# Gated MLP with linear attention on one core: gates of two token chunks kept in SBUF, tiles from any of three pools, refitted tables

## The chip, the core and the metric

The kernel runs on one core of a Trainium2 chip. The metric is the device time of one execution in microseconds (us). The core has five engines with a queue each: TensorE (PE in the profile; its weight loads are PEld), VectorE (DVE), ScalarE (ACT), GpSimd (POOL) and SyncE (SP), which here does nothing but issue DMAs. ScalarE issues some DMAs too.

## The reference

With S = 2048 tokens, width D = 640, 32 heads of 20, and F = 1536:

```python
xn = layernorm(x)
q, k, v = split_heads(xn @ wqkv)
phi = lambda t: concat([softmax(t @ w_phi), softmax(-(t @ w_phi))])    # per head
o = phi(q) @ (phi(k).T @ v) / (phi(q) @ phi(k).sum(tokens) + 1e-6)
s = merge_heads(o) @ wo
g = silu(gelu(xn @ w1 + b1) @ w2 + b2)
out = x + s * g
```

All in fp32. The output is written transposed, D rows by S columns.

## The kernel before

Every fp32 operand of a matmul is kept as a high and a low half (tiles of shape P x 2 x n), and a product is three matmuls over these halves (`PASSES`). Making the low half means one subtraction: "bank" copies the source to PSUM by ScalarE and subtracts on VectorE from PSUM; "vector" subtracts on VectorE from SBUF; "pool" on GpSimd from SBUF. The tokens are four chunks (c = 0 to 3) of CW = 512 columns, the output rows five blocks (d = 0 to 4) of 128.

The stages by the profiled execution's span: projections and the kv state to about 240 us; then `up` for chunks 2 and 3 (UP0) to 313, `down(2)` for the same chunks (DN0) to 396, `up` for chunks 0 and 1 (UP1) to 471, `down(0)` (DN1) to 550, and the output stage (OUT) to 648. Both MLP products are in Strassen-like forms: block sums of hr and of w2 are multiplied and the products added with signs. `form` (L1428) makes the operand hs of a product from the gelu results hr, six steps ahead; `step` calls it.

From UP0 on the order of every instruction is written out by hand: a counter of slots goes up with each `tick`, and `when`, `soon` and `after` put a call into a slot. The numbers come from the table `PLAN`. UP0, DN0, UP1, DN1 and OUT begin at slots 0, 42, 84, 126 and 168. A number like 165.25 is slot 165, behind what stands at 165.0 there. Each engine then works through its own queue in that order, and SyncE's queue holds most DMAs: a DMA that has to wait for its data holds back every DMA behind it on that queue.

In `down`, `gate_out` finishes a block of the MLP: it adds on VectorE what is needed (L1333), applies Silu on ScalarE (L1544) into a tile y, and a store to `g_dram` is issued on SyncE (all DMAs through `load` have line L1353). In the output stage `gate(i)` (L1789) loads the block back into a tile gt from the pool "cells". `load_res` (L1784) loads the matching block of x into xres.

In between, the attention's q side is prepared per token tile of 128 (16 tiles, four to a chunk), as `plan_q` orders it: `q_load` (eq), `q_ez` on GpSimd (L1667), `q_rc` (L1671), `q_dn`, which is a chain of six instructions on VectorE (L1677 to L1684), `q_scale` on GpSimd (L523), two transposes on VectorE (L1695) into a tile pt, and `q_put2`, which stores pt to `phi_dram` in four DMAs per half. `get_phi` loads them back as six tiles ph per chunk. `num_step` (six calls per chunk; num(c) below) multiplies these by the kv state (L1747, L1755) into PSUM banks, and ScalarE and VectorE write the halves of oT (L1751, L1752, and for the sixth part oTl L1760, L1761). A `spread`, a DMA of 32 KB on ScalarE's queue (L1764), moves a part of oTl into each of the five oT tiles.

`finish(c, d)` takes 15 matmuls of oT and wo per tile (L1815), multiplies gt by the bank on VectorE (L1817, two halves), adds xres on GpSimd (L1818; on VectorE for the last two tiles), and a store to the output follows.

Tiles come from pools with a fixed number of buffers: "slabs" (10), "cells" (21), "halves" (6), "late" (13, opened after UP1) and "phs" (1). A new tile of a pool waits for the readers of the tile that had its buffer. Before the change every kind of tile has one pool: oT, oTl, gt and hs come from cells, q tiles from late once it is open, and ph from late or slabs by the chunk (`c_ph`).

Of the kernel before, what the change touches and what calls it, by code (L numbers as in the profile page):

```python
# [15 lines left out]
P = 128  # L16
# [25 lines left out]
def _ft(t):  # L42
# [27 lines left out]
        [26.75, 31.75, 34.25, 35, 40],  # L70
        [38, 40, 43.0, 44, 45],
# [3 lines left out]
        [41.5, 41.5],  # L75
        [40, 42],
        [40.5, 45.25],
        [38, 43.5],
        [40.75, 45.5],
        [71.75, 74.0],  # L80
        [66, 73],
        [71.5, 76],
        [35, 35.5],
        [35.5, 37.5],
        [37.75, 38.75],
# [6 lines left out]
        [135.5, 156],  # L92
# [51 lines left out]
    "phi": [
        [152.5, 153.75, 158.0, 160.5, 160.0, 158.0],
        [161.5, 166.6, 161.7, 169.3, 169.9, 169.0],
        [176.5, 176.6, 176.7, 177.8, 174.9, 179.0],
        [184.25, 187.6, 187.7, 187.8, 187.9, 191.0],
    ],
    "num": [165.25, 173.5, 184.75, 194.25],  # L150
    "res": [166.25, 164, 171.25, 172.5, 172, 175.25, 175.5, 176.75, 184, 180.5, 180.5, 186, 186, 194, 191.75, 193.75, 195.75, 200, 196.5, 202],
    "gate": [167.1, 167.1, 168.1, 170.1, 168.6, 172.1, 176.1, 178.1, 180.1, 182.1, 185.1, 183.1, 190.85, 190.1, 192.1, 194.1, 195.1, 200.1, 199.1, 200.6],
    "c_ph": ['late', 'slab', 'late', 'slab'],
    "st": [3, 3, 4.75, 3, 4, 3, 3, 3, 3, 3, 3, 3, 5, 4, 4, 6, 3, 3, 3.75, 3],
    "c_st": ['scalar', 'sync', 'sync', 'sync', 'sync', 'sync', 'sync', 'sync', 'sync', 'sync', 'sync', 'scalar', 'scalar', 'sync', 'sync', 'sync', 'sync', 'scalar', 'sync', 'scalar'],
# [4 lines left out]
def hedgehog_gated_mlp_kernel(ctx: ExitStack, tc: tile.TileContext, x, xt_in, wqk, bd, wv, wo, w1, b1, w2, b2, out_t):  # L160
# [31 lines left out]
    open_psum(early_psum, A=3, T=1)  # L192
# [3 lines left out]
    def slab(dt, name, shape=(P, 2, D)):  # L196
        pool = slabs if next(homes, "S") == "S" else lead
        return pool.tile(list(shape), dt, tag="S", name=name)
# [939 lines left out]
    o = 7  # L1138
# [183 lines left out]
    halves = ctx.enter_context(tc.tile_pool(name="halves", bufs=6, reuse_waits="tile"))  # L1322
    ffn = ExitStack()
    ffn.enter_context(tc.manual_schedule())

    def cell(shape, dt, name):
        return cells.tile(list(shape), dt, tag="C", name=name)

    def half(name, shape=(P, CW)):
        return halves.tile(list(shape), F32, tag="U", name=name)  # L1330

    def add(out, a, b, eng=nc.vector, op=OP.add):
        eng.tensor_tensor(out, a, b, op=op)  # L1333
# [115 lines left out]
    W2AT = dict(A11=0, A21=2 * P, A12=4 * P, A22=6 * P, A5=8 * P)  # L1449
    SUMS = ("S2", "S3", "S4", "S1")  # L1450
# [78 lines left out]
    def down(c0, los):  # L1529
# [197 lines left out]
    def get_phi(c, n):  # L1727
        assert {("phi", c, u, h) for u in range(2) for h in range(2)} <= seen
        j = (5, 0, 1, 2, 3, 4)[n]
        if j == 5:  # L1730
            t = tailp[1].tile([P, CW], F32, tag="H", name="ph")
            load(t[:80], phi_dram[c, 1200:])
        else:
            w = PLAN["c_ph"][c]
            t = (cell((P, 2, CW), F32, "ph") if w == "cell" else
                 slab(F32, "ph", (P, 2, CW)) if w == "slab" else tall(F32, "ph", (P, 2, CW)))
            load(t[:], phi_rows(c, 240 * j))
        phis[c][j] = t
# [43 lines left out]
    xres, gates, wo_s, wo_r = {}, {}, [], []  # L1782
# [6 lines left out]
    def gate(i):  # L1789
        c, d = divmod(i, KC)  # L1790
        assert ("g", d, c) in seen
        gates[c, d] = cell((P, CW), F32, "gt")
        nc.sync.dma_start(gates[c, d][:], g_dram[d][:, c])
# [186 lines left out]
```

## Time and profile before

| | us |
|---|---|
| median of 3 runs | 649.2 (648.74 to 651.68) |
| the profiled execution's own time | 649.97 |
| its span | 648.1 |
| mean granted TensorE clock | 0.996 |
| TensorE busy | 625.4 |
| DMA moved | 155.26 MB, mean 240 GB/s |

The rows of the profile name an engine, a line of the kernel, the operation, "out<-in" with the names of tiles, and partitions x elements. In a timeline a row has its start, its length, how many instructions were joined in it (x12), and in brackets how long the engine sat idle before it and what ended that. In the table of waits a row has the sum, the number of times and the longest.

### The profile page before, as it was taken

How to read it: one execution, taken by the hardware profiler on the slowest of the kernel's cores; microseconds unless marked ns; L12 is line 12 of the kernel's file. 1: busy time of each engine (PE TensorE's matmuls, PEld its weight loads, DVE VectorE, ACT ScalarE, POOL GpSimd, SP SyncE). 2: the span in 40 equal slices, each digit the busy share in tenths (PEclk: the TensorE clock that was granted, in tenths of full speed). 3: DMA queues.
4: the chain of work that ended last, by engine and by line, in shares of the span. 5: the costliest groups of instructions: out<-in, count | busy, mean ns of one | idle time of the engine just before them, and what ended most of it. 6: DMA issues, size and time to landing. Idle time of an engine off the chain costs nothing.

```text
span 648.1 us, 11723 instructions
## 1 busy us (share of the span) xinstructions
PE 625.4 (97%) x4288; PEld 538.8 (83%) x4288; DVE 460.1 (71%) x706; ACT 365.8 (56%) x639; POOL 440.6 (68%) x390
## 2 busy tenths in 40 slices
PE   8999999999999999999989899999999999799997
PEld 8999999999899998888768688888788886466666
DVE  5878997766785767746688966889889973753242
ACT  4556877754476769877977476342597474121020
POOL 3597887775775439987799785666679977332332
PEclk9999999999999999999999999999999999989999
DMA  8436822132723858998999899967476998999974
GB/s 322 190 104 223 268 71 83 42 103 83 223 80 124 300 204 306 364 329 305 304 411 268 241 322 373 413 194 210 116 235 213 340 324 284 279 286 311 305 252 176
DMA packets 129609, 155.26 MB, mean 240 GB/s; under 512 B 48176, under 2 KB 89648, under 8 KB 129040
## 3 DMA queue, kind: packets, MB, share of 16 engines
q1 hardware_dynamic: 128656, 152.81, 70.7%
q10 hardware_dynamic: 896, 1.70, 0.7%
q8 instruction: 34, 0.56, 0.4%
q14 instruction: 23, 0.19, 0.1%
HBM read 98.96 MB, written 53.54 MB: 235 GB/s over the span
## 4 chain that ended last, share of the span: by engine, by line
PE 64%; POOL 12%; DMA 11%; issue 3%; DVE 3%; SPq 3%; ACT 2%; POOLq 0%
PE pB L1312 21%; PE pW L606 20%; PE pB L1523 6%; PE pB L1815 6%; PE pA L465 4%; POOL hr L1425 4%; DMA out_dram<-xres 3%; PE pW L1089 3%; DMA ph<-phi_dram 2%; POOL ez L1667 2%; SPq L1353 2%; DMA xp<-xp_dram 2%; PE pA L284 2%; DMA eq<-e_dram 1%; POOL eq L523 1%
## 5 line engine op out<-in xcount | busy, mean ns | idle before, releaser
L1523 PE MATMUL pB<-hs,w2s 128*128 128x512 f32 x648 | 149.1, 390 | 5.1 <-DVE hs L1443 2.9
L1523 PEld LDWEIGHTS pB<-hs,w2s 128*128 128x128 f32 x648 | 121.2, 188 | 32.8 <-DVE hs L1443 3.3
L1312 PE MATMUL pB<-xp,w1s 128*128 128x512 f32 x324 | 79.8, 390 | 0.8 <-DVE pB L1333 0.8
L1312 PE MATMUL pB<-xd,w1s 128*128 128x512 f32 x324 | 79.4, 389 | 0.0
L1815 PE MATMUL pB<-oT,wo 128*128 128x512 f32 (+1 forms) x315 | 70.7, 383 | 2.1 <-DMA oT<-oTl 2.1
L1312 PEld LDWEIGHTS pB<-xp,w1s 128*128 128x128 f32 x324 | 60.7, 188 | 13.8 <-DVE pB L1333 1.2
L1815 PEld LDWEIGHTS pB<-oT,wo 128*128 128x128 f32 x315 | 56.3, 188 | 18.1 <-issue 6.0
L1312 PEld LDWEIGHTS pB<-xd,w1s 128*128 128x128 f32 x324 | 60.8, 188 | 12.5
L1818 POOL TENSOR_TENSOR xres<-gt,xres 128x256 f32<-128x256 f32 x36 | 25.6, 735 | 59.3 <-DVE gt L1817 49.3
L1380 ACT ACTIVATE hr<-pB,b1t 128x512 f32<-128x512 f32 x48 | 32.6, 687 | 52.0 <-DVE pB L1333 51.6
L504 POOL TENSOR_TENSOR e<-e,mxs 128x1280 f32<-128x1280 f32 x12 | 28.8, 2408 | 40.4 <-DVE mxs L499 36.0
L1443 DVE TENSOR_TENSOR hs<-pB,hs 128x512 fp32r<-128x512 f32 x59 | 39.0, 679 | 19.0 <-ACT hs L1439 19.0
L1439 ACT ACTIVATE hs<-hr 128x512 fp32r<-128x512 f32 x84 | 50.7, 622 | 3.1 <-DMA s_dram<-ws 1.7
L1438 ACT ACTIVATE pB<-hr 128x512 f32<-128x512 f32 x59 | 34.9, 592 | 24.4 <-DVE rc L1684 12.6
L510 ACT ACTIVATE e<-e 128x1280 f32<-128x1280 f32 x32 | 40.7, 1273 | 13.6 <-POOL e L504 5.7
L606 PE MATMUL pW<-wsum,xd 128*128 128x320 f32 x288 | 48.4, 310 | 0.0
L1425 POOL TENSOR_TENSOR hr<-hr 128x512 f32<-128x512 f32 x36 | 47.5, 1346 | 1.2 <-DVE hs L1443 1.1
L606 PEld LDWEIGHTS pW<-wsum,xd 128*128 128x128 f32 x288 | 43.6, 188 | 0.0
L1817 DVE TENSOR_TENSOR gt<-pB,gt 128x256 f32<-128x256 f32 x40 | 15.2, 418 | 38.7 <-PE pB L1815 28.9
L523 POOL TENSOR_TENSOR e<-e,rc 128x1280 f32<-128x1280 f32 x15 | 36.1, 2409 | 5.8 <-DVE rc L950 4.3
L1667 POOL TENSOR_TENSOR ez<-eq,zrep 128x1280 f32<-128x1280 f32 x12 | 35.5, 2961 | 5.5 <-DMA eq<-e_dram 5.5
L1333 DVE TENSOR_TENSOR pB<-u,pB 128x512 f32<-128x512 f32 x36 | 24.7, 687 | 12.0 <-PE pB L1312 11.7
(244 smaller groups left out, 1366.2 us busy)
## 6 DMA issues: line engine op xcount, KB each, us to landing
w2s<-s_dram SPq DMA_DIRECT2D x24, 512.0 KB
e_dram<-e SPq DMA_DIRECT2D x16, 640.0 KB
ph<-phi_dram SPq DMA_DIRECT2D x20, 512.0 KB
raw<-in_w_dram SPq DMA_DIRECT2D x24, 320.0 KB
eq<-e_dram SPq DMA_DIRECT2D x12, 640.0 KB
phi_dram<-pt SPq DMA_DIRECT2D x48, 160.0 KB
w_dram<-w1s SPq DMA_DIRECT2D x12, 512.0 KB
s_dram<-ws SPq DMA_DIRECT2D x12, 512.0 KB
```

The costliest lines, as they stand in the source:

```text
L510: nc.scalar.activation(ef, ef, AF.Exp)
L523: eng.tensor_tensor(e3, e3, rc[:, :, None].to_broadcast([P, 64, DH]), op=OP.mult)
L606: nc.tensor.matmul(self.bank[ch][:, :HALF], self.x(blk, a), w(b), start=new and i == 0, stop=i == len(mms) - 1, skip_group_check=True)
L1312: nc.tensor.matmul(bank[ch][:], tl[:, a, off + wo_:off + wo_ + P], mov(blk, b), start=new and n == 0, stop=n == len(mms) - 1, skip_group_c ...
L1380: nc.scalar.activation(dst, ps, AF.Gelu_apprx_tanh, bias=b1t[:, f:f + 1])
L1425: nc.gpsimd.tensor_tensor(block(k, g), block(a, g), block(b, g), op=OP.subtract)
L1438: nc.scalar.activation(ps[:], src, AF.Copy)
L1439: nc.scalar.activation(hs[:, 0], src, AF.Copy)
L1443: (nc.gpsimd if lo == "pool" else nc.vector).tensor_tensor(hs[:, 1], ps[:] if lo == "bank" else src, hs[:, 0].bitcast(F32), op=OP.subtract)
L1523: nc.tensor.matmul(ps[:], w(b), hs[:, a, :], start=start and n == 0, stop=stop and n == 2, skip_group_check=True)
L1667: nc.gpsimd.tensor_tensor(qz[t], qe[t], zf[0], op=OP.mult)
L1815: nc.tensor.matmul(ps[:, cols], w, o[:, a, cols], start=n == 0, stop=n == 14)
```

## The change

1. Gates of chunks 0 and 1 stay in SBUF. `gate_out` with c0 == 0 writes its sums and Silu into one of five tiles ys (P x 2 x CW, one per d), and `gate` has nothing to load for c < 2. Ten stores to `g_dram` and ten loads from it, of 256 KB each, are no longer there, and `finish` multiplies into ys. The five tiles take their room from late, which has 9 buffers for 13.
2. Pools as rings. `from_ring` takes the first of several pools whose oldest tile is no longer held by the program that writes the instructions; ph, oT, gt, and the q tiles use it.
3. `PLAN` is refitted: slots of nearly all kinds, and for some tiles which engine makes the low half. In the first list of `lo` (the forms of DN0) entry 10 goes from bank to vector and entry 18 from pool to vector; in the second (DN1) entry 17 from vector to bank and entry 33 from pool to bank.

```diff
+    class Ring:
+        def tile(self, shape, dt, name, tag=None):
+            t = Tile(self.pool.tile(list(shape), dt, tag=self.tag, name=name))
+            self.given.append(weakref.ref(t))
+            return t
+        def ready(self):
+            return len(self.given) < self.n or self.given[-self.n]() is None
+    def from_ring(names, shape, dt, name):
+        names = [n for n in names if n in rings]
+        for n in names:
+            if rings[n].ready():
+                return rings[n].tile(shape, dt, name)
+        return rings[names[0]].tile(shape, dt, name)
...
         def gate_out(d, o, src, plus=None, late=1):
+            if c0 == 0:
+                if d not in ys:
+                    ys[d] = tailp[2].tile([P, 2, CW], F32, tag="Y", name="ys")
+                y = gates[o, d] = ys[d][:, o]
+                if plus is not None:
+                    add(y, src, plus)
+                    src = y
+                nc.scalar.activation(y, src, AF.Silu, bias=b2t[:, d:d + 1])
+                return
             y = half("y")
...
     def tall(dt, name, shape=(P, 2, D)):
-        if tailp:
-            return tailp[0].tile(list(shape), dt, tag="L", name=name)
-        return slab(dt, name, shape)
+        return from_ring(("late", "slab"), shape, dt, name)
...
     def new_oT():
-        return [cell((P, 2, 512), F32R, "oT") for _ in range(5)], cell((P, 2, 512), F32R, "oTl")
+        return [from_ring(("cell", "slab", "late"), (P, 2, 512), F32R, "oT") for _ in range(5)], cell(
+            (P, 2, 512), F32R, "oTl")
...
     def gate(i):
         c, d = divmod(i, KC)
-        assert ("g", d, c) in seen
-        gates[c, d] = cell((P, CW), F32, "gt")
-        nc.sync.dma_start(gates[c, d][:], g_dram[d][:, c])
+        if c >= 2:
+            assert ("g", d, c) in seen
+            t = from_ring(("cell", "slab", "late"), (P, CW), F32, "gt")
+            nc.sync.dma_start(t[:], g_dram[d][:, c])
+            gates[c, d] = t[:]
...
-    "num": [165.25, 173.5, 184.75, 194.25],
+    "num": [163.75, 173.5, 185.0, 194.25],
...
-    tailp.append(ctx.enter_context(tc.tile_pool(name="late", bufs=13, side="right", reuse_waits="tile")))
+    tailp.append(ctx.enter_context(tc.tile_pool(name="late", bufs=9, side="right", reuse_waits="tile")))
+    rings["late"] = Ring(tailp[0], 9, "L")
     tailp.append(ctx.enter_context(tc.tile_pool(name="phs", bufs=1, side="right", reuse_waits="tile")))
+    tailp.append(ctx.enter_context(tc.tile_pool(name="ys", bufs=5, side="right", reuse_waits="tile")))
```

How the order moves is shown at three places. First SyncE's queue at the end of DN1 and the beginning of OUT, before; L1353 is any load or store through `load`, L1787 the load of x, L1793 the load of a gate:

```order
L1353 DMA ph<-phi_dram 80x512
L1353 DMA ph<-phi_dram 128x2x512
L1353 DMA g_dram<-y 128x512 x3
L1787 DMA xres<-in_xt_dram 128x512 x2
L1353 DMA phi_dram<-pt_5978 32x20x64 x4
...
L1353 DMA g_dram<-y 128x512 x2
L1793 DMA gt<-g_dram 128x512 x4
L1353 DMA ph<-phi_dram 128x2x512 x3
L1793 DMA gt<-g_dram 128x512
```

And after, where L1387 stands for L1353 and L1830 for L1787:

```order
L1387 DMA ph<-phi_dram 80x512
L1387 DMA ph<-phi_dram 128x2x512
L1387 DMA phi_dram<-pt_5990 32x20x64 x4
L1830 DMA xres<-in_xt_dram 128x512 x2
L1387 DMA ph<-phi_dram 128x2x512 x3
L1383 DMA out_dram<-xres 128x512
L1830 DMA xres<-in_xt_dram 128x512 x3
```

The five stores of y and the first four gate loads no longer stand between the stores of pt_5978 (now pt_5990) and the three ph loads that follow.

Second, TensorE from DN1 into OUT, before: L1523 are the products of down, L1755 and L1747 those of num, L1815 those of the output:

```order
L1523 MATMUL pB<-hs,w2s 128x512 x312
L1755 MATMUL pB<-ph,bdl 40x256 x2
L1747 MATMUL pB<-ph,bdk 64x512 x10
L1523 MATMUL pB<-hs,w2s 128x512 x12
L1815 MATMUL pB<-oT,wo 128x512 x38
...
L1815 MATMUL pB<-oT,wo 128x512 x82
...
L1815 MATMUL pB<-oT,wo 128x512 x75
```

And after, with L1558, L1797, L1789 and L1860 for these four:

```order
L1558 MATMUL pB<-hs,w2s 128x512 x300
L1797 MATMUL pB<-ph,bdl 40x256 x2
L1789 MATMUL pB<-ph,bdk 64x512 x10
L1558 MATMUL pB<-hs,w2s 128x512 x24
L1860 MATMUL pB<-oT,wo 128x512 x38
...
L1860 MATMUL pB<-oT,wo 128x512 x90
...
L1860 MATMUL pB<-oT,wo 128x512 x67
```

num(0) stands 12 matmuls earlier, num(1) where it was, and num(2), between the 90 and the 67, 8 matmuls later.

Third, VectorE in DN0, where u is copied from the first product's bank, before:

```order
L1468 TENSOR_TENSOR w2s<-pB,w2s 128x2x256 x2
L1677 TENSOR_REDUCE pB<-qroom 128x64
L1680 SCALAR_TENSOR_TENSOR pB<-rc,pB 128x32
L1681 TENSOR_TENSOR pB<-pB,rc 128x64
L1682 TENSOR_REDUCE pB<-pB 128x32
L1683 RECIPROCAL pB<-pB 128x32
L1684 TENSOR_TENSOR rc<-rc,pB 128x64
L1566 COPY u_4140<-pB 128x512
L1443 TENSOR_TENSOR hs<-pB,hs 128x512
```

And after, with L1610 for the copy, L1719 to L1726 for the chain and L1477 for the forms:

```order
L1503 TENSOR_TENSOR w2s<-pB,w2s 128x2x256
L1610 COPY u_4130<-pB 128x512
L1477 TENSOR_TENSOR hs<-hr,hs 128x512
L1719 TENSOR_REDUCE pB<-qroom 128x64
L1722 SCALAR_TENSOR_TENSOR pB<-rc,pB 128x32
L1723 TENSOR_TENSOR pB<-pB,rc 128x64
L1724 TENSOR_REDUCE pB<-pB 128x32
L1725 RECIPROCAL pB<-pB 128x32
L1726 TENSOR_TENSOR rc<-rc,pB 128x64
```

The copy of u moved from behind the chain `q_dn` to ahead of it, and the form that follows reads both its operands from SBUF (hr), where before it read one from PSUM.

More of the change, by code (lines that the diff above doesn't have):

```diff
@@ L1 @@
+import weakref
 from contextlib import ExitStack
@@ L74 @@
         [34.5, 34.75],
-        [41.5, 41.5],
-        [40, 42],
+        [38.5, 39.5],
+        [40, 41],
         [40.5, 45.25],
[L78 to L83, printed above, removed]
+        [41, 43.5],
+        [40.25, 48.75],
+        [72.25, 74.5],
+        [60.5, 73.5],
+        [72.25, 76.0],
+        [35, 36.5],
         [35.5, 37.5],
-        [37.75, 38.75],
+        [33.75, 40.25],
         [118.5, 121.25],
@@ L91 @@
         [129, 131.5],
-        [135.5, 156],
+        [133.5, 154],
         [146.0, 150.0],
@@ L131 @@
     "c_w1": ['pool', 'bank', 'pool', 'bank', 'vector', 'bank', 'bank', 'bank', 'bank', 'vector', 'pool', 'pool'],
-    "c_w10": ['pool', 'dve', 'pool', 'dve', 'dve', 'dve', 'dve', 'bank', 'dve', 'bank', 'pool', 'bank', 'bank', 'pool', 'pool', 'bank', 'pool', 'bank', 'dve', 'dve'],
+    "c_w10": ['pool', 'dve', 'pool', 'dve', 'dve', 'dve', 'dve', 'bank', 'dve', 'bank', 'pool', 'dve', 'bank', 'pool', 'pool', 'bank', 'dve', 'bank', 'dve', 'dve'],
     "qend": [63.0],
     "put": [
-        [57.5, 59.6],
+        [57.0, 59.1],
@@ L136 @@
         [64.0, 64.1],
-        [101.5, 102.6],
-        [112.5, 111.6],
-        [120.5, 120.85],
+        [102.0, 103.1],
+        [112.0, 111.1],
+        [123.5, 121.85],
         [139.5, 139.6],
-        [155.5, 166.6],
-        [174.75, 175.85],
+        [156.5, 168.35],
+        [174.25, 175.85],
     ],
     "phi": [
[L145 to L148, printed above, removed]
-    ],
@@ L150 @@
-    "num": [165.25, 173.5, 184.75, 194.25],
[L151 to L155, printed above, removed]
+        [152.5, 153.75, 156.0, 160.5, 160.0, 158.0],
@@ new lines @@
+        [165.75, 167.85, 163.45, 169.55, 170.15, 169.25],
+        [176.5, 176.6, 176.7, 177.8, 172.9, 179.0],
+        [183.25, 186.6, 186.7, 186.8, 186.9, 190.0],
+    ],
+    "num": [163.75, 173.5, 185.0, 194.25],
+    "res": [168.5, 168.5, 171.25, 172.5, 172, 174.25, 175.5, 176.75, 184, 180.5, 180.5, 186, 186, 194, 191.75, 193.75, 195.75, 197, 196.5, 202],
+    "gate": [167.1, 166.85, 168.1, 171.1, 168.6, 171.1, 176.35, 178.1, 179.6, 182.1, 185.1, 183.1, 190.85, 190.1, 192.1, 194.1, 195.1, 200.1, 199.1, 199.6],
@@ L191, in hedgehog_gated_mlp_kernel, with __init__, __getitem__, __getattr__ @@
     open_psum(kv_psum, K=1)
-    open_psum(early_psum, A=3, T=1)
+    open_psum(early_psum, T=1, A=3)
+    class Tile:
+        def __init__(self, t):
+            self.t = t
+        def __getitem__(self, i):
+            return self.t[i]
+        def __getattr__(self, n):
+            return getattr(self.t, n)
+    class Ring:
+        def __init__(self, pool, n, tag):
+            self.pool, self.n, self.tag, self.given = pool, n, tag, []
+        def tile(self, shape, dt, name, tag=None):
[4 more added lines that the diff above has]
+            return len(self.given) < self.n or self.given[-self.n]() is None
+    rings = {"slab": Ring(slabs, 10, "S")}
+    def from_ring(names, shape, dt, name):
[4 more added lines that the diff above has]
+        return rings[names[0]].tile(shape, dt, name)
     homes = iter(HOMES)
     def slab(dt, name, shape=(P, 2, D)):
-        pool = slabs if next(homes, "S") == "S" else lead
-        return pool.tile(list(shape), dt, tag="S", name=name)
+        if next(homes, "S") == "S":
+            return rings["slab"].tile(shape, dt, name)
+        return lead.tile(list(shape), dt, tag="S", name=name)
     def row(shape, dt, name):
@@ L1322, in hedgehog_gated_mlp_kernel @@
     halves = ctx.enter_context(tc.tile_pool(name="halves", bufs=6, reuse_waits="tile"))
+    rings["cell"] = Ring(cells, 21, "C")
     ffn = ExitStack()
@@ L1326, in cell @@
     def cell(shape, dt, name):
-        return cells.tile(list(shape), dt, tag="C", name=name)
+        return rings["cell"].tile(shape, dt, name)
     def half(name, shape=(P, CW)):
@@ L1734, in get_phi @@
             w = PLAN["c_ph"][c]
-            t = (cell((P, 2, CW), F32, "ph") if w == "cell" else
-                 slab(F32, "ph", (P, 2, CW)) if w == "slab" else tall(F32, "ph", (P, 2, CW)))
+            t = from_ring({"cell": ("cell", "slab", "late"), "slab": ("slab", "cell", "late"),
+                           "late": ("late", "slab", "cell")}[w], (P, 2, CW), F32, "ph")
             load(t[:], phi_rows(c, 240 * j))
@@ L1801, in split_wo @@
         j = len(wo_s)
-        wo_s.append(split_w(wo_r[j][:], "wo", "pool", tailp[0]))
+        wo_s.append(split_w(wo_r[j][:], "wo", "pool", rings["late"]))
     def finish(c, d, oT, last):
```

54 lines of the change are left out of this document (29 added, 25 removed), and 6 rows, old and new, of the table PLAN.

## Prediction

> **What bounds the kernel now.** I read the page first, then TensorE's waits, then the timelines around the longest waits. The page's first line says which engine carries the span:
>
> ```profile
> PE 625.4 (97%) x4288; PEld 538.8 (83%) x4288; DVE 460.1 (71%) x706; ACT 365.8 (56%) x639; POOL 440.6 (68%) x390
> ```
>
> TensorE is busy for 625.4 of 648.1 us, and the change leaves its matmuls as they are. So the time can move only by what TensorE waits for, by the clock that it gets, and by the tail. The table of its waits (us in total, times, longest):
>
> ```profile
> PE pB L1747 <- DMA ph<-phi_dram: 5.0, 2, 4.1
> PE pB L1523 <- DVE hs L1443: 2.9, 1, 2.9
> PE pB L1815 <- DMA oT<-oTl: 2.1, 5, 0.8
> PE pB L1523 <- DVE u L1566: 1.7, 1, 1.7
> ...
> PE pB L1312 <- DVE pB L1333: 0.8, 1, 0.8
> ```
>
> These five rows are 12.5 us, all in stages whose order the change touches. The largest is the wait for phi, in the output stage. TensorE's timeline there (start, length, tile, count, idle before and its releaser):
>
> ```profile
> 546.87 3.02 PE L1523 MATMUL pB<-hs,w2s 128*128 128x512 f32 x12
> 550.74 0.93 PE L1815 MATMUL pB<-oT,wo 128*128 128x512 f32 x3 [0.85 <-DMA oT<-oTl]
> 552.01 2.37 PE L1815 MATMUL pB<-oT,wo 128*128 128x512 f32 x9 [0.34 <-DMA oT<-oTl]
> 554.67 6.16 PE L1815 MATMUL pB<-oT,wo 128*128 128x512 f32 x26 [0.28 <-DMA oT<-oTl]
> ...
> 561.22 1.89 PE L1747 MATMUL pB<-ph,bdk 120*64 120x512 f32 x8
> 567.19 4.49 PE L1747 MATMUL pB<-ph,bdk 120*64 120x512 f32 x12 [4.08 <-DMA ph<-phi_dram]
> 571.61 18.92 PE L1815 MATMUL pB<-oT,wo 128*128 128x512 f32 x82
> ...
> 590.93 4.46 PE L1747 MATMUL pB<-ph,bdk 120*64 120x512 f32 x20
> ```
>
> The work of down ends at 546.87 + 3.02 = 549.89; I call this point H and count from it. num(1), the numerator of chunk 1, stops after 8 of its 20 L1747 matmuls for 4.08 us. Why the tile came late stands in SyncE's timeline and, behind it, in the chain that ended last:
>
> ```profile
> 542.69 0.81 SPq L1353 DMA_DIRECT2D ph<-phi_dram x2
> 543.60 1.41 SPq L1353 DMA_DIRECT2D g_dram<-y  x3
> ...
> 554.10 0.94 SPq L1353 DMA_DIRECT2D g_dram<-y  x2
> 555.13 4.46 SPq L1793 DMA_DIRECT2D gt<-g_dram  x4
> 559.64 1.45 SPq L1353 DMA_DIRECT2D ph<-phi_dram  x3
> ```
>
> ```profile
> 554.10 4.62 DMA g_dram<-y
> ...
> 560.12 6.94 DMA ph<-phi_dram
> ```
>
> SyncE issues in order. The last three ph loads of chunk 1 stand behind two stores of y, which can only start when the last products of down are through Silu, and behind four gate loads, the first of which waits for a store to land. So they are issued at H+9.8 and land at H+17.2, where TensorE wanted the first of them at about H+13.2.
>
> **The change part by part, output stage.** The 20 stores and loads that go are 10 x 256 KB each way. What they cost is not their bytes but their place in this queue. The order of after has, on SyncE, the three ph loads directly behind the phi_dram stores and two xres loads: nothing in front of them waits for H any more. They still wait for the semaphore lanes of eight issues earlier. I put the landing at H+9, worked out from the 6.94 us of one such load and an issue at about H+2. num(1) still starts behind 38 output matmuls (38 x 18.92/82 = 8.8 us) and needs its last three tiles at H + 8.8 + 0.6 + 2 x 0.89 = H+11.2 and after. So the 4.08 goes, with a margin of about 2 us.
>
> With it goes a loss of clock. 12 matmuls after that wait took 4.49 us; 20 of the same took 4.46 without one, which is 2.7 for 12. The difference is 1.8 us. Shorter waits lost nothing; these two rows, of the first down stage, are used again below:
>
> ```profile
> 334.14 30.25 PE L1523 MATMUL pB<-hs,w2s 128*128 128x512 f32 x132 [1.67 <-DVE u L1566]
> 367.31 28.89 PE L1523 MATMUL pB<-hs,w2s 128*128 128x512 f32 x126 [2.92 <-DVE hs L1443]
> ```
>
> Both runs of matmuls go at 229 ns each (30.25/132, 28.89/126). So the clock's term is 1.8 for the 4.08 and nothing for waits up to 2.92; what lies between is not shown here.
>
> num(0) stands 12 matmuls earlier in TensorE's order (24 of down behind it instead of 12). That gives the five spreads of oT 12 x 0.25 = 3.0 us more cover, from the 3.02 us row. The waits of 0.85, 0.34 and 0.28 at chunk 0's first tile, 1.5 in all, go.
>
> What is late next? For chunk 1 it is the way from num(1) to the first output tile at H + 8.8 + 5.1 + 37 x 0.23 = H+22.4 (num(1): 4.46 from the row above and some 0.6 for its four short matmuls). VectorE and GpSimd have to finish the last two q tiles first, and VectorE's queue puts the oTl of chunk 1 behind them. VectorE, then GpSimd, then ScalarE before:
>
> ```profile
> 552.63 1.28 DVE L1333 TENSOR_TENSOR y<-pB,u 128x512 f32<-128x512 f32 x2
> 553.83 1.48 DVE L1671 TENSOR_REDUCE rc<-eq 128x64 f32<-128x1280 f32 x1
> ...
> 560.87 0.75 DVE L1817 TENSOR_TENSOR gt<-pB,gt 128x256 f32<-128x256 f32 x2
> ...
> 566.59 2.48 DVE L1695 STREAM_TRANSPOSE pt<-eq 128x640 f32<-128x640 f32 x3
> 568.99 0.37 DVE L1761 TENSOR_TENSOR oTl<-pB,oTl 40x256 fp32r<-40x256 f32 x1
> ```
>
> ```profile
> 561.42 1.41 POOL L1818 TENSOR_TENSOR xres<-gt,xres 128x256 f32<-128x256 f32 x2 [11.61 <-DVE gt L1817]
> 562.79 4.67 POOL L523 TENSOR_TENSOR eq<-eq,rc 128x1280 f32<-128x1280 f32 x2
> ```
>
> ```profile
> 550.53 1.40 ACTq L1764 DMA_DIRECT2D oT<-oTl  x2
> ...
> 572.28 0.61 ACTq L1764 DMA_DIRECT2D oT<-oTl  x1
> ...
> 576.61 1.24 ACTq L1764 DMA_DIRECT2D oT<-oTl  x2
> ```
>
> In after's order VectorE does, from H: y (1.3), two rc (2 x 1.48), a q_dn chain (2.9, from the rows of DN0 below), a gate product (0.75), the second chain (2.9), another product (0.75). GpSimd has xres (1.41), eq (4.67/2), xres, eq, and starts with the first product's end at about H+8. It ends at H + 8 + 2 x 1.41 + 4.67 = H+15.5. A transpose follows, then oTl at H+16 to H+17 (before: 568.99, H+19.1). The spreads are issued 3.3 to 7.6 us after oTl, as before (572.28 and 576.61 against 568.99), that is up to H+24, and land about 3.3 us later: at chunk 0 the last of two was issued by 551.4, and TensorE's third wait for oT ended at 554.67. TensorE needs the five oT tiles from H+22.4 to H+25.1. A new wait at chunk 1's first tile is the likeliest result: 0.3 to 3.3 us. I take 2.0, the upper middle, because the chain has no slack step in it. It is under 2.92, so no clock term.
>
> Chunks 2 and 3: num(2) stands 8 matmuls later, which takes 8 x 0.23 = 1.8 us of cover from its spreads, while their lanes see fewer transfers; the rest of the oT row (2.1 - 1.5 = 0.6) I halve to 0.3. The second ph wait (5.0 - 4.1 = 0.9) goes: its loads are due a slot earlier and two gate loads leave the queue before it. Tail: chunk 3 is done as before, so 0. Output stage: -1.5 - 4.1 - 1.8 + 2.0 - 0.9 - 0.3 = **-6.6 us**.
>
> **The change part by part, first down stage (DN0).** VectorE's rows around both waits of 1.67 and 2.92:
>
> ```profile
> 333.40 0.68 DVE L1566 COPY u<-pB 128x512 f32<-128x512 f32 x1
> ...
> 354.00 6.41 DVE L1443 TENSOR_TENSOR hs<-hr,hs 128x512 fp32r<-128x512 f32 x1
> 360.34 0.68 DVE L1443 TENSOR_TENSOR hs<-pB,hs 128x512 fp32r<-128x512 f32 x1
> 360.94 1.48 DVE L1677 TENSOR_REDUCE pB<-qroom 128x64 f32<-128x1280 f32 x1
> ...
> 366.43 0.22 DVE L1684 TENSOR_TENSOR rc<-rc,pB 128x64 f32<-128x64 f32 x1
> 366.57 1.28 DVE L1443 TENSOR_TENSOR hs<-pB,hs 128x512 fp32r<-128x512 f32 x2
> ```
>
> The copy of u stood behind a q_dn chain of 2.9 us (two of them take 360.94 to 366.65); in after's order it stands ahead of it. The 1.67 goes but for some 0.3: -1.4. The 2.92 has two causes in a row: hs<-hr took 6.41 us, where its group's median is 1.12, and then two chains stood ahead of the hs that TensorE waited for:
>
> ```profile
> L1443 DVE TENSOR_TENSOR hs<-hr,hs x13: 669/1123/6409, 307.9 to 533.0; 128x512 fp32r<-128x512 f32 x13
> ```
>
> In after one hs stands between the two chains, which would help, but the refit makes two more of this kind (entry 10 from bank, entry 18 from pool) in the same stage, and what stretched the 6.41 was GpSimd working without a pause through it. I take -0.6 for this wait; bounds are -2.9 and, with one more such stretch (6.41 - 1.12 = 5.3) half hidden, +2.6. DN0: **-2.0 us**.
>
> UP1's 0.8 (a sum of VectorE behind a chain; the order around it changes) I halve: -0.4. The other table entries (earlier weight and x loads, w1 forms moved to VectorE) lie in stages where no row above shows TensorE waiting; the cover is TensorE's 97%, and without it a form of 128x512 costs 0.7 to 1.1 us. I take 0. The rings choose pools when the program is written; they cost no instruction.
>
> Sum: -6.6 - 2.0 - 0.4 = -9.0. The profiled execution took 649.97 us (648.1 of span and 1.9 around it), which is 0.8 above the median of 649.2 and inside the runs' 648.74 to 651.68. 649.97 - 9.0 = **641.0 us**; I don't take off the 0.8, since new small waits are likelier than new savings.
>
> **The rivals.** First, *the wait moves*: the chain through VectorE and GpSimd ends where my bound ends, chunk 1's first tile waits 3.3 us in one piece and the clock falls too (1.8): 641.0 - 2.0 + 3.3 + 1.8 = 644.1 us. For it: the chain is serial, H+15.5 at best. Against: the five tiles arrive one by one, so the wait comes in pieces. Chance 0.17. [...]
>
> Second, *the transfers are late anyway*: a ring gives a tile whose last reader is already written, not already run, or the lanes stay full, and the ph loads still miss. Then only 1.5 + 2.0 + 0.4 is gained: 646.1 us. For it: the load itself took 6.94 us, so it has little to give. Against: five stores and four loads leave the queue ahead of it. Chance 0.10.
>
> Third, *slower*: VectorE's two new SBUF-to-SBUF forms in DN0 are held by GpSimd as the 6.41 was. There GpSimd has long runs without a pause (in after's order three ez and six hr in one piece). Two stretches of 5.3 and a clock loss are 12.4 us: 653.4 us. It decides from 9.0 us of new waiting on. Against: it was one of 13, with a median of 1.12, and the change takes one such form off GpSimd. Chance 0.09. [...]
>
> **How the numbers follow.** The forecast has the remaining 0.64. Its low end: no wait at chunk 1 (-2.0), all of DN0's 4.6 (-2.6), all of UP1 (-0.4) and of chunk 2 (-0.3): 635.7. The high end takes in the first two rivals and DN0 without its gain on the second: 646.1 + 2.0 = 648.1. Range 635.5 to 648. A measurement of this kernel can tell about 0.5%, 3.2 us. Below 645.95 lie the forecast, most of the first rival and a third of the second: 0.78. Within 0.5%: 0.14. Above 652.4: most of the third, 0.08.
>
> **What would show it.** Right: no wait of L1747's kind at num(1); SyncE's three ph loads issued by H+3; chunk 1's first output matmuls waiting for oT<-oTl by 0.3 to 3.3 us; the u copy ahead of its chain and no 1.67. Wrong: TensorE still stopping in num(1); a wait of over 3.3 us at chunk 1; or VectorE rows hs<-hr over 4 us in DN0 with TensorE idle behind them.

## The result, and the profile after

The changed kernel takes 643.29 us (median of 6 runs, 638.55 to 645.92) against 649.55 us before (6 runs, 648.74 to 651.68): a ratio of 0.9894, 95% interval 0.9856 to 0.9931. The profiled execution took 643.78 us, its span 642.0. The forecast was 641.0 in a range of 635.5 to 648. An execution more than 1.5% above the fastest of its kernel is left out of the medians and ratios of the runs below: one each of after_again (654.75 us), num_back (657.96) and thin_in_place (659.44).

TensorE's waits after (us in total, times, longest):

```profile
PE pB L1558 <- DVE hs L1477: 5.5, 5, 1.9
...
PE pB L1860 <- DMA oT<-oTl: 1.1, 3, 0.7
...
PE pB L1319 <- DVE w2s L1503: 0.9, 1, 0.9
```

The row of L1747 for phi (5.0) is gone, and oT halved. In its place the products of down wait for hs: 5.5 us in five pieces, where before it was 2.9 in one. Where the time went is seen best by stages. From the first matmul of each stage to the first of the next (OUT to TensorE's last; a wait in front of OUT's first matmul is counted to OUT), in us:

| stage | before | after | difference | forecast |
|---|---|---|---|---|
| up to DN0 | 313.2 | 313.0 | -0.1 | 0 |
| DN0 | 82.9 | 82.3 | -0.5 | -2.0 |
| UP1 | 74.9 | 73.8 | -1.1 | -0.4 |
| DN1 | 78.8 | 82.8 | +4.0 | 0 |
| OUT | 94.5 | 85.8 | -8.6 | -6.6 |
| TensorE's last matmul to the span's end | 3.9 | 4.2 | +0.3 | 0 |

So the sum of 9.0 became 6.1 in the span, by errors of both signs: OUT gave 2.0 more than forecast and UP1 0.7 more, DN0 gave 1.5 less, and DN1, to which the forecast gave no term, took 4.0 away. That the time came out within 2.3 us of the forecast is in part luck, since these errors partly cancel.

TensorE's timeline after, from DN1 on (start, length, tile, count, idle before it):

```profile
512.51 29.13 PE L1558 MATMUL pB<-hs,w2s 128*128 128x512 f32 x118 [1.92 <-DVE hs L1477]
541.58 0.63 PE L1797 MATMUL pB<-ph,bdl 80*40 80x256 f32 x4
542.04 4.46 PE L1789 MATMUL pB<-ph,bdk 120*64 120x512 f32 x20
546.43 5.74 PE L1558 MATMUL pB<-hs,w2s 128*128 128x512 f32 x24
552.01 2.90 PE L1860 MATMUL pB<-oT,wo 128*128 128x512 f32 x12
555.06 6.16 PE L1860 MATMUL pB<-oT,wo 128*128 128x512 f32 x26 [0.15 <-DMA oT<-oTl]
561.15 0.63 PE L1797 MATMUL pB<-ph,bdl 80*40 80x256 f32 x4
561.61 4.46 PE L1789 MATMUL pB<-ph,bdk 120*64 120x512 f32 x20
566.00 20.70 PE L1860 MATMUL pB<-oT,wo 128*128 128x512 f32 x90
```

H is 546.43 + 5.74 = 552.17. num(1) runs in one piece (20 matmuls in 4.46), chunk 0's first tile waits 0.15 in place of 1.5, and the 90 matmuls behind num(1), in which chunk 1's first tile begins, have no wait in them. SyncE's queue at that place:

```profile
552.93 1.13 SPq L1830 DMA_DIRECT2D xres<-in_xt_dram  x2
554.11 1.63 SPq L1387 DMA_DIRECT2D ph<-phi_dram  x3
```

The three ph loads are issued from H+1.9 to H+3.6; before it was H+9.8. And VectorE in DN1, with GpSimd beside it:

```profile
503.28 1.27 DVE L1367 TENSOR_TENSOR u<-u,pB 128x512 f32<-128x512 f32 x2
504.48 7.98 DVE L1477 TENSOR_TENSOR hs<-hr,hs 128x512 fp32r<-128x512 f32 x1
512.38 1.48 DVE L1719 TENSOR_REDUCE pB<-ez 128x64 f32<-128x1280 f32 x1
```

```profile
502.33 2.96 POOL L1709 TENSOR_TENSOR ez<-eq,zrep 128x1280 f32<-128x1280 f32 x1
505.25 2.53 POOL L1459 TENSOR_TENSOR hr<-hr 128x512 f32<-128x512 f32 x2
507.75 1.28 POOL L1477 TENSOR_TENSOR hs<-hr,hs 128x512 fp32r<-128x512 f32 x1
509.00 2.91 POOL L1709 TENSOR_TENSOR ez<-eq,zrep 128x1280 f32<-128x1280 f32 x1
515.42 2.37 POOL L556 TENSOR_TENSOR eq<-eq,rc 128x1280 f32<-128x1280 f32 x1 [3.52 <-DVE rc L1726]
```

The form of 7.98 us ends at 512.46, where GpSimd's last instruction of an unbroken row had ended at 511.91. GpSimd stopped there only because its next step needed VectorE's rc. TensorE waited 1.92 us for hs. It is a form that the kernel before has too, as vector (entry 22 of the second list); there it took 2.25 us.

### The profile page after: what moved, and what is told of

Same layout as the page of the kernel before. It is cut to its first block, busy times and chain, and to the rows that moved or that the text cites. A ratio compares the mean times of both kernels' runs of the same rounds, so it can differ in the third digit from the quotient of the medians.

```text
span 642.0 us, 11695 instructions
## 1 busy us (share of the span) xinstructions
PE 625.2 (97%) x4288; PEld 539.6 (84%) x4288; DVE 465.2 (72%) x709; ACT 366.0 (57%) x639; POOL 437.5 (68%) x387
## 4 chain that ended last, share of the span: by engine, by line
PE 69%; DMA 10%; POOL 7%; DVE 6%; issue 4%; ACT 2%; SPq 1%; ACTq 0%; DVEq 0%; POOLq 0%
PE pB L1345 21%; PE pW L639 21%; PE pB L1558 10%; PE pB L1860 5%; PE pA L498 4%; PE pW L1122 3%; DVE hs L1477 3%; POOL hr L1459 2%; DMA out_dram<-xres 2%; DMA qroom<-e_dram 2%; PE pA L317 2%; DMA gt<-g_dram 1%; PE kv L731 1%; DMA oT<-oTl 1%; POOL qroom L556 1%
## 5 line engine op out<-in xcount | busy, mean ns | idle before, releaser
L1558 PE MATMUL pB<-hs,w2s 128*128 128x512 f32 x648 | 151.7, 394 | 5.6 <-DVE hs L1477 5.5
L1558 PEld LDWEIGHTS pB<-hs,w2s 128*128 128x128 f32 x648 | 121.9, 190 | 35.0 <-DVE hs L1477 7.7
L1860 PE MATMUL pB<-oT,wo 128*128 128x512 f32 (+1 forms) x315 | 70.2, 381 | 1.1 <-DMA oT<-oTl 1.1
L1860 PEld LDWEIGHTS pB<-oT,wo 128*128 128x128 f32 x315 | 56.7, 188 | 15.8 <-issue 3.6
L1477 DVE TENSOR_TENSOR hs<-pB,hs 128x512 fp32r<-128x512 f32 x60 | 39.5, 678 | 12.1 <-ACT hs L1473 12.1
L556 POOL TENSOR_TENSOR eq<-eq,rc 128x1280 f32<-128x1280 f32 x12 | 28.5, 2372 | 11.4 <-DVE rc L1726 11.4
L1863 POOL TENSOR_TENSOR xres<-ys,xres 128x256 f32<-128x256 f32 x20 | 14.1, 739 | 24.3 <-DMA xres<-in_xt_dram 12.5
```

The costliest lines, as they stand in the source:

```text
L556: eng.tensor_tensor(e3, e3, rc[:, :, None].to_broadcast([P, 64, DH]), op=OP.mult)
L1477: (nc.gpsimd if lo == "pool" else nc.vector).tensor_tensor(hs[:, 1], ps[:] if lo == "bank" else src, hs[:, 0].bitcast(F32), op=OP.subtract)
L1558: nc.tensor.matmul(ps[:], w(b), hs[:, a, :], start=start and n == 0, stop=stop and n == 2, skip_group_check=True)
L1860: nc.tensor.matmul(ps[:, cols], w, o[:, a, cols], start=n == 0, stop=n == 14)
```

## The experiments

Theory A at the outset: OUT's gain is the place of the gates' DMAs in SyncE's queue, and DN1's loss is a race between VectorE and GpSimd for the reads of one instruction. Rival B: the refitted slots make the gain, and DN1's loss is VectorE's load. Ratios are to the kernel before, run on the same chip, with 95% intervals; stage lengths are those of the profiled execution, taken as in the table above. The runs were made on three chips, four rows of the table on each, where the kernel before took 650.7, 649.6 and 649.5 us; so a difference of medians between two of these groups is uncertain by about 1 us.

| run | median us | ratio | DN0 | DN1 | OUT |
|---|---|---|---|---|---|
| after_again | 643.07 | 0.9898 (0.9858 to 0.9939) | 82.4 | 82.8 | 85.2 |
| dn1_bank | 638.81 | 0.9817 (0.9785 to 0.9850) | 81.8 | 78.5 | 85.5 |
| gates_back | 651.52 | 1.0016 (0.9993 to 1.0040) | 82.7 | 78.5 | 97.7 |
| num_back | 641.63 | 0.9889 (0.9845 to 0.9932) | 82.5 | 78.5 | 87.8 |
| thin_in_place | 644.67 | 0.9923 (0.9893 to 0.9952) | 82.7 | 78.5 | 93.1 |
| late_transfers | 653.82 | 1.0067 (1.0046 to 1.0087) | 82.2 | 78.5 | 100.4 |
| dn0_undo | 643.19 | 0.9895 (0.9871 to 0.9919) | 87.1 | 78.5 | 86.3 |
| dn0_bank | 638.63 | 0.9824 (0.9795 to 0.9854) | 81.1 | 78.5 | 86.8 |
| before_ph_first | 652.76 | 1.0045 (1.0028 to 1.0061) | 84.7 | 78.8 | 98.2 |
| before_bank | 647.52 | 0.9967 (0.9948 to 0.9985) | 81.5 | 78.8 | 94.9 |
| num_back_bank | 642.61 | 0.9890 (0.9869 to 0.9911) | 82.4 | 78.5 | 88.4 |
| no_ring | 643.25 | 0.9900 (0.9883 to 0.9918) | 82.8 | 78.5 | 88.7 |

**DN1's long form.** The run after_again is the changed kernel itself.

> The changed kernel once more, unaltered, to see what of its spread (638.55 to 645.92 us in six runs) comes back. Theory A: the one long form in down of chunks 0 and 1 (hs<-hr on VectorE, 7.98 us in the first profile) is a race that VectorE wins or loses from run to run; its length in this profile can be anything from 1 to 8 us, and the output stage looks the same (no wait for ph). Median 640 to 645. Rival B: the stall is fixed by the order; the row comes back within 0.5 us of 7.98.

The long form is back with 7.99 us, so B's sign came true in this run. The answer is in the other traces: in num_back the order on VectorE and GpSimd is the same to the instruction, in gates_back there only the gates' tile has another name, and in both the form took 1.36 us. In num_back:

```profile
504.69 1.36 DVE L1477 TENSOR_TENSOR hs<-hr,hs 128x512 fp32r<-128x512 f32 x1
```

```profile
502.53 2.97 POOL L1709 TENSOR_TENSOR ez<-eq,zrep 128x1280 f32<-128x1280 f32 x1
505.44 3.02 POOL L1459 TENSOR_TENSOR hr<-hr 128x512 f32<-128x512 f32 x2
```

The same three instructions; here the form ended at 506.05, 0.55 us behind the end of the ez (505.50), and GpSimd's two sums took 3.02 instead of 2.53. In after five GpSimd instructions ended beside the form, and it ended 0.55 us behind the last of them (511.91), where GpSimd paused. In both traces the form begins at the same place, 2.15 us (after) and 2.16 us (num_back) behind the start of the ez. In these four traces it is one or the other: 7.98 and 7.99, or 1.36 and 1.36. The next run takes one of the form's operands out of SBUF:

```diff
     "lo": [
...
-    (second list, entry 22)  "vector"
+    (second list, entry 22)  "bank"
```

> The changed kernel with entry 22 of the second lo list made from bank in place of vector: the form that took 7.98 us reads one operand from PSUM. Theory A: its row is then about 0.7 us, the wait of 1.92 and the 2.2 us of lost clock behind it go, the median is 2 to 4 us below the changed kernel's and the spread narrower. Rival B: VectorE is simply full in this stretch (two chains and seven forms); the wait comes back behind the next chain with 1 us or more, and the median moves by less than 1.5 us.

A, and by more than expected: 638.81 us, 4.3 below the changed kernel's 643.07 on the same chip, and five executions lie within 637.34 to 639.46. DN1 is 78.5 us here, as in every run of a changed table without the long form, and 4.3 less than with it. VectorE was not too full. This version, one word of a table away, beats both kernels.

**The gates.** The gates of chunks 0 and 1 go through `g_dram` again, with the gate slots of the kernel before:

```diff
         def gate_out(d, o, src, plus=None, late=1):
-            if c0 == 0:
-                ...
-                return
...
     def gate(i):
-        if c >= 2:
-            assert ("g", d, c) in seen
...
+        assert ("g", d, c) in seen
+        t = from_ring(("cell", "slab", "late"), (P, CW), F32, "gt")
```

> The changed kernel with the gates of chunks 0 and 1 stored to g_dram and loaded again as before (gate slots of before, all other tables of after). Theory A: SyncE's queue holds the ph loads of chunk 1 behind stores and gate loads again; num(1) waits for ph 2 to 5 us, with clock loss behind it if the wait is 3 us or more; the output stage is 4 to 7 us longer than the changed kernel's. Rival B: the refitted slots of phi and num do it, not the gates; num(1) waits less than 1 us and the time is within 2 us of the changed kernel's.

OUT is 97.7 us, 12.2 more than dn1_bank's with the gates in SBUF and even 3.2 more than before the change: the refitted slots without the kept gates are worse than the old ones. A, beyond its range of 4 to 7.

```profile
559.11 1.94 PE L1780 MATMUL pB<-ph,bdk 120*64 120x512 f32 x8 [1.05 <-DMA ph<-phi_dram]
568.84 5.61 PE L1780 MATMUL pB<-ph,bdk 120*64 120x512 f32 x12 [7.79 <-DMA ph<-phi_dram]
```

The prediction said that not the bytes but the place in the queue is what the DMAs cost. Two runs part these. The first keeps 20 DMAs at the places of gates_back, with 16 columns each:

```diff
+                after(late, load, g_dram[d][:, o, :16], ys[d][:, o, :16])
...
+        t = from_ring(("cell", "slab", "late"), (P, CW), F32, "gt")
+        nc.sync.dma_start(t[:, :16], g_dram[d][:, c, :16])
```

> The kernel of dn1_bank (gates in SBUF), with 20 DMAs at the queue places that the gates of chunks 0 and 1 had in gates_back, but of 8 KB each (16 columns; what they carry is not used). Place without bytes. Theory A (the place in SyncE's queue and on the lanes): num(1) waits for ph again, 3 us or more, and the time is 5 us or more above dn1_bank's 638.8. Rival B (the 5.2 MB): the thin transfers land at once, num(1) waits less than 1.5 us, the time is within 2.5 us of 638.8.

A: with 8 KB each the wait is nearly as long as with 256 KB (6.95 against 7.79 us), and the time is 5.9 us above dn1_bank. But OUT is 93.1 us here and 97.7 with the full transfers at the same places: of the 12.2 us, 4.6 come only with the full transfers. TensorE, then SyncE:

```profile
566.07 4.29 PE L1795 MATMUL pB<-ph,bdk 120*64 120x512 f32 x12 [6.95 <-DMA ph<-phi_dram]
```

```profile
537.57 0.89 SPq L1387 DMA_DIRECT2D ph<-phi_dram  x2
549.70 0.93 SPq L1387 DMA_DIRECT2D g_dram<-ys  x2
550.73 0.86 SPq L1848 DMA_DIRECT2D gt<-g_dram  x2
551.68 1.43 SPq L1387 DMA_DIRECT2D ph<-phi_dram  x1
...
558.36 0.89 SPq L1387 DMA_DIRECT2D ph<-phi_dram  x2
```

SyncE stands for 11 us, from 538.46 to 549.70, before a store that needs the end of down; all that is behind it moves by that. The second run keeps the bytes, behind the ph loads of chunk 1 (what they carry is not used):

```diff
     def gate(i):
...
+        load(g_dram[d][:, c], wo_s[d][:, 0, :CW].bitcast(F32))
+        after(3, again, c, d)
...
+    def again(c, d):
+        t = from_ring(("cell", "slab", "late"), (P, CW), F32, "gt")
+        nc.sync.dma_start(t[:], g_dram[d][:, c])
```

> The kernel of dn1_bank with the 20 transfers of 256 KB put back (what they carry is not used), but behind the ph loads of chunk 1 in SyncE's queue, five slots later. Bytes without the place. Theory A: num(1) does not wait; chunk 2's and 3's ph, x and gate loads are pushed a little, 0 to 3 us in all; 638.8 to 642. Rival B (the bytes): the output stage is 5 us or more longer, by waits for DMAs.

num(1) has no wait, as A said, but the time is 15 us above dn1_bank, which is B's number. The waits are in chunks 1 and 2. The largest is of a spread of chunk 2; TensorE, ScalarE, then SyncE:

```profile
605.92 12.04 PE L1867 MATMUL pB<-oT,wo 128*128 128x512 f32 x45 [4.87 <-DMA oT<-oTl]
```

```profile
599.69 0.59 ACTq L1806 DMA_DIRECT2D oT<-oTl  x1
600.38 0.60 ACT L1793 ACTIVATE oT<-pB 128x512 fp32r<-128x512 f32 x1 [13.10 <-DMA out_dram<-xres]
```

```profile
593.65 3.29 SPq L1845 DMA_DIRECT2D gt<-g_dram  x2
```

ScalarE stood for 13.10 us, most of it at the issue of a spread. The bracket names the last of several waits; by the semaphores in the trace, the issue waited for one of the loads that the edit put back (L1845), which SyncE had issued only at 593.65 and which landed at 599.62. The DMAs that SyncE and ScalarE issue signal on eight semaphores in turn (433 DMAs in this trace, 54 or 55 on each), and an issue waits until the DMA eight issues ahead of it has landed; the prediction calls these lanes. So it is a queue again, and these transfers were not free at this place either. The third run moves the ph loads in the kernel before, and nothing else:

```diff
     "phi": [
...
-        [161.5, 166.6, 161.7, 169.3, 169.9, 169.0],
+        [161.5, 166.6, 161.7, 166.92, 166.93, 166.91],
```

> The kernel before, with one row of its table changed: the last three ph loads of chunk 1 are written ahead of the last two stores of y and of the gate loads. No transfer less. Theory A (place): num(1)'s wait of 4.08 and the clock behind it go or fall below 1 us, part of it comes back later in the stage through the gate loads that are now later; 643 to 647 us. Rival B (bytes): the ph loads are issued earlier but land late all the same, or the gates now hold up the finish of chunk 0 for as long; the time is within 2 us of the kernel before.

Against A, and worse than B's number: 3.2 us slower than before (0.45%), where B had it within 2. The way is the second that B named. num(1)'s wait of 4.08 is gone, but chunk 0's finish now waits for the gates, and so does everything behind it (the profiled execution took 655.17 us, of which 1.8 more than before are in DN0, which the edit doesn't touch):

```profile
571.96 8.66 PE L1815 MATMUL pB<-oT,wo 128*128 128x512 f32 x30 [2.21 <-DVE gt L1817]
581.81 10.80 PE L1815 MATMUL pB<-oT,wo 128*128 128x512 f32 x45 [1.19 <-DMA oT<-oTl]
...
607.26 1.68 PE L1815 MATMUL pB<-oT,wo 128*128 128x512 f32 x6 [0.80 <-DMA oT<-oTl]
...
624.17 1.08 PE L1747 MATMUL pB<-ph,bdk 120*64 120x512 f32 x4 [1.48 <-DMA ph<-phi_dram]
```

**num(0), and the rings.** num(0) back at its slot, first in the changed kernel, then in dn1_bank's:

```diff
-    "num": [163.75, 173.5, 185.0, 194.25],
+    "num": [165.25, 173.5, 185.0, 194.25],
```

> The changed kernel with num(0) at its old slot, 12 matmuls of down behind it instead of 24; nothing else moves on any engine. Theory A: chunk 0's first tile waits for oT<-oTl again, 1.2 to 2.5 us in all, and the time rises by that. Rival B: the spreads land sooner now that SyncE's stores are gone; the waits stay under 0.6 us and the time moves by less than 0.5 us.

> The kernel of dn1_bank with num(0) at its old slot: the run num_back once more, without the form whose length changes from run to run. In that trace chunk 0's first tile waited 1.96 us in three pieces. Theory A: 1.3 to 2.2 us above dn1_bank's 638.8. Rival B: less than 0.6 us, since chunk 1 then has as much less to wait for.

In num_back the waits of chunk 0's first tile are 1.24, 0.39 and 0.33 us, but the median (641.63) says nothing, since the changed kernel's long form comes and goes. Without that form num_back_bank is 3.8 us slower than dn1_bank: A's sign and more than A's size. Of the 3.8, OUT's 2.9 are 1.8 more at chunk 0 (1.25, 0.43 and 0.26 us for 0.16) and small waits at chunk 2; the rest lies in stages that the edit doesn't touch. The rings always give their first pool:

```diff
     def from_ring(names, shape, dt, name):
         names = [n for n in names if n in rings]
-        for n in names:
-            if rings[n].ready():
-                return rings[n].tile(shape, dt, name)
         return rings[names[0]].tile(shape, dt, name)
```

> The kernel of dn1_bank with from_ring always giving the first pool that it is asked for (oT and gt from cells, q tiles from late with its 9 buffers, ph from slabs). The order of the instructions is the same on every engine; only which buffer a tile gets differs. Theory A: with four buffers less in late, q tiles and the loads into them wait for readers, SyncE is held in the second down stage, and TensorE waits for ph or oT at num(0) or num(1): 3 us or more longer. Rival B: the pools never were full where it matters; within 1 us of 638.8.

It costs 4.4 us, A's number, but not by A's way. No q tile or ph holds TensorE; chunk 0's first tile waits for a spread:

```profile
553.04 8.93 PE L1857 MATMUL pB<-oT,wo 128*128 128x512 f32 x32 [2.73 <-DMA oT<-oTl]
```

Here SyncE issues chunk 1's ph loads at 546.21, before H (548.95), and chunk 0's spreads are issued from 543.62 to 549.31, at the same time; in after the loads came at H+1.9. That the two collide is argued, not shown.

**DN0.** Entries 10 and 18 as before the change, then entries 10, 18 and 22 all from bank, both on dn1_bank:

```diff
     "lo": [
-    (first list, entries 10 and 18)  "vector", "vector"
+    (first list, entries 10 and 18)  "bank", "pool"
```

> The kernel of dn1_bank with entries 10 and 18 of the first lo list as before the change (bank, pool). The forecast gave the first down stage 2.0 us of gain, the first trace showed 0.1. Theory A: the two forms on VectorE (2.75 and 2.08 us in the traces, against 0.68 from bank) eat what the moved copy of u saves; undone, the first down stage is 0.5 to 2 us shorter. Rival B: they cost nothing, the chains of VectorE do; the stage is within 0.4 us, or longer, since GpSimd gets one form more.

```diff
     "lo": [
-    (first list, entries 10, 18 and 22)  "vector", "vector", "vector"
+    (first list, entries 10, 18 and 22)  "bank", "bank", "bank"
```

> The kernel of dn1_bank with entries 10, 18 and 22 of the first lo list from bank: none of the three long forms of the first down stage reads both operands from SBUF. Theory A: VectorE gets about 4 us back (2.75 + 2.08 + 1.73 - 3 x 0.68), TensorE's waits for hs there (3.5 us in four) fall below 1.5, and the median is 636 to 638, below all others. Rival B: the two chains and the transposes are the bound; the waits stay above 2.5 us and the time is 638.5 to 640.

Undone, the time is 4.4 us longer, against A. TensorE waits in one piece, for GpSimd:

```profile
356.59 43.45 PE L1558 MATMUL pB<-hs,w2s 128*128 128x512 f32 x178 [7.69 <-POOL hs L1477]
```

With the refitted slots entry 18 on GpSimd stands behind a row of sums and an ez and comes too late: so entry 18 had to move. In the same trace entry 22's form on VectorE took 7.78 us, against 1.75 in dn1_bank, so the long form is bound neither to DN1 nor to one table. dn0_bank's DN0 is 0.7 us shorter than dn1_bank's and its waits for hs fall from 3.5 to 2.0, but the medians are the same (638.63 and 638.81); the gain is below what these runs can tell. In the profiled execution a wait of 1.75 that is left in DN0 also cost clock (granted 0.51 from 354 to 356 us). The same word in the kernel before, in both lists:

> The kernel before with entry 22 of both lo lists from bank in place of vector: the form that took 6.41 us in the first down stage, and its fellow in the second (2.24 us). Theory A: TensorE's wait of 2.92 for hs goes below 0.7 and the time falls by 2 to 3.5 us. Rival B: the two chains behind it are enough for the wait; it stays above 1.5 us and the time is within 1.2 us of the kernel before.

2.0 us less (0.33%, interval 0.15 to 0.52), at the lower end of A: the wait of 2.92 in DN0 is gone, and DN0 is 1.4 us shorter. The form of 6.41 us was needed for that wait; the two chains behind it were not enough. DN0 is shorter by less than the 2.92 because the wait of 1.66 for u, which cost no clock before, cost some here (granted 0.50 from 334 to 336 us).

## Why the prediction came out as it did

*Chunk 0's oT, -1.5.* Right, with 0.15 left. num_back_bank shows that it is the 12 matmuls' cover, and that they are worth more (2.9 in OUT).

*The ph wait and its clock, -4.1 and -1.8.* Right in place and size: no wait is left, and both thin_in_place (6.95) and gates_back (7.79) bring it back. The step "what they cost is not their bytes but their place in this queue" failed in its first half. thin_in_place shows the place, but the full transfers at the same places cost 4.6 us more of OUT, and late_transfers and before_ph_first show two other places that cost as much or more. No run with the full transfers had a shorter OUT than the kernel before.

*Chunk 1's new wait, +2.0.* This term failed: 0. The chain itself was right. After, ScalarE and VectorE:

```profile
570.28 0.57 ACTq L1806 DMA_DIRECT2D oT<-oTl  x1
...
572.96 1.85 ACTq L1806 DMA_DIRECT2D oT<-oTl  x2
```

```profile
568.12 0.37 DVE L1803 TENSOR_TENSOR oTl<-pB,oTl 40x256 fp32r<-40x256 f32 x1
```

oTl starts at H+16.0, as worked out. But the first spread follows it by 2.2 us, not by 3.3, and the last is issued by 6.7, where before it was 8.9 (the 7.6 of the prediction is the start of a row of two): they no longer stand at a lane; before, ScalarE sat 2.05 us there, for an xres load. The last is issued by H+22.6 and the fifth oT is needed at H+25.1. I had carried a delay over from a queue that the change empties. This is the first rival's premise too.

*Chunks 2 and 3, -0.3 and -0.9.* The second is right. The first has the wrong sign: 0.66 and 0.32 remain of oT there, for 0.6 before. As measured, the terms of OUT make 7.7 (1.3 + 5.9 + 0.9 - 0.4) of its 8.6; the other 0.9 is not assigned.

*DN0, -2.0.* It was -0.5. The copy of u is ahead of its chain and the 1.67 is gone, but four waits for hs (0.74, 0.72, 1.54, 0.54) took the place of the 2.92. What I called the price of the two new forms was paid (2.75 and 2.08 us against 0.68 from bank), without any long stretch.

*UP1, -0.4.* It was -1.1; the wait of 0.8 is gone whole, where I had halved it.

*DN1, 0.* This is the step that failed in the sum: no row showed a wait of TensorE there, and I took the cover for granted. The third rival had a form held beside GpSimd, but for two new forms in DN0 and as something that a new form brings. The form that was hit is an old one, and before it took 2.25 us and ended at 507.61, 0.55 behind the end of an ez. The traces of before and after have 27 forms with both operands in SBUF. Beside 19 of them a GpSimd instruction ended; these took 0.78 to 7.98 us, and each ended 0.55 us behind such an end. The other 8 took 0.67 to 0.69. In 17 of the 19 it was the first end beside the form; the exceptions are the 7.98, with five ends, and the 6.41 of before, with four. There VectorE's row ends at 360.41, and GpSimd's rows are:

```profile
351.92 2.55 POOL L1425 TENSOR_TENSOR hr<-hr 128x512 f32<-128x512 f32 x2
354.43 2.95 POOL L1667 TENSOR_TENSOR qroom<-qroom,zrep 128x1280 f32<-128x1280 f32 x1
357.33 2.54 POOL L1425 TENSOR_TENSOR hr<-hr 128x512 f32<-128x512 f32 x2
363.91 2.36 POOL L523 TENSOR_TENSOR qroom<-qroom,rc 128x1280 f32<-128x1280 f32 x1 [4.04 <-DVE rc L1684]
```

In both it ended only where GpSimd paused (3.52 us in after, 4.04 here), and so did the 7.78 of dn0_undo (3.51). With one operand from PSUM the form of 7.98 took 0.68 us, beside the same ez (dn1_bank, 502.73 to 503.41). That the two engines contend for reads of SBUF is my reading of these rows; by what rule the form comes through at the first end or only at a pause was not shown.

*The clock, "nothing for waits up to 2.92".* This failed as well, and with it the 3 us from which gates_back's expectation counts a clock loss: in other executions waits of 1.66 to 2.88 us cost clock; see the last section.

## What to carry to other kernels

When a queue issues in order, look for the DMA that waits longest for its data: thin or thick, it delayed everything behind it here (TensorE waited 6.95 us with 8 KB each, 7.79 with 256 KB), and moving its neighbours only moved the wait (before_ph_first, 3.2 us slower), so the gain lies in not needing the DMA. A delay read from a queue that the change empties may not be carried into the forecast. And a form of VectorE with both operands in SBUF had no fixed length beside a busy GpSimd in these traces (0.78 to 7.99 us): take its worst one (here 8 us, not the median of 1.1) when asking whether TensorE is covered, or let it read one operand from PSUM (0.65 to 0.69 us in all 119 such forms of before and after).

## What the runs showed of the hardware

The same wait of 1.92 us cost clock in one execution and none in the other. The columns are the stretch, its length, busy time (and instructions) of PE, PEld, DVE, ACT, POOL, then the granted clock, DMA share and GB/s; after first, then after_again:

```profile
512.00:514.00 2.00, 1.49 (x5) 1.21 (x6) 1.97 (x3) 0.00 (x0) 0.00 (x0) 0.77 1.04 402
514.00:516.00 2.00, 2.00 (x6) 1.59 (x5) 1.86 (x7) 0.63 (x2) 0.58 (x1) 0.50 1.08 387
516.00:518.00 2.00, 2.00 (x9) 1.36 (x7) 2.00 (x3) 1.57 (x3) 2.00 (x2) 0.88 0.22 86
```

```profile
514.00:516.00 2.00, 2.00 (x10) 1.66 (x9) 1.86 (x7) 0.68 (x2) 0.63 (x1) 1.00 1.01 374
```

In after the clock was halved for 3.41 us and DN1's 118 matmuls took 29.13 us, 2.3 more than at 0.2275 each (the rate of the 182 ahead of them, 41.41 us). In after_again the clock stayed at 1.00; TensorE was faster, came to the next hs too early and waited 1.45 us there, so DN1 has the same length in both (82.8). The waits of 1.54 (after) and 2.92 (before) in DN0 cost nothing (granted 1.00 behind both), those of 4.08 and 7.79 did (12 matmuls of num(1) in 4.49 and 5.61 us, against 2.7 at the rate of num(0)'s 20 in 4.46). In before_ph_first the wait of DN0 was 2.88 and cost clock: 126 matmuls in 30.36 us, against 28.89 behind the 2.92. So did waits of 1.66 (before_bank, granted 0.50; its fellow of 1.67 in before did not, granted 1.00), 1.75 (dn0_bank, 0.51), 2.21 (before_ph_first, 30 matmuls in 8.66 us, against 7.10 in gates_back) and 2.73 (no_ring, 32 in 8.93 us, where 26 took 6.16 in after). All waits from 3.29 us on cost clock: behind 3.29 (late_transfers), 3.99 (before_bank) and 6.95 (thin_in_place) 12 matmuls of num took 5.75, 5.39 and 4.29 us, behind 4.87 (late_transfers) 45 of the output took 12.04, against 10.53 in after, and behind 7.69 (dn0_undo) 178 of down took 43.45, 2.7 more than at 0.229 each. In the clock records of the fourteen traces there are 13 halved stretches up to TensorE's last matmul, and each is 3.41 us long or two or three times that (one of 3.41 in before and one in after). So in these executions waits between 1.66 and 2.92 us cost clock in some cases and not in others, and the length alone does not say which. What decides it was not shown.
